# Float64 weights assembled with one more ScalarE pass and two VectorE passes, and zero products placed before TensorE work that the planner sees starting late

## The chip, the cores and the metric

The kernel runs on one NeuronCore of one Trainium2 chip. The metric is the device time of one execution in microseconds. TensorE (PE) multiplies matrices into PSUM, VectorE (DVE) and ScalarE (ACT) work elementwise on SBUF and PSUM, GpSimd (POOL) computes and issues indirect DMAs, SyncE (SP) issues most plain DMAs. Each engine takes its instructions in program order and waits for the others by semaphores.

## The reference, cut to what matters

```
# x (8,8,512,64), state (8,8,32,64) float32: attention in both directions
xread = softmax(x @ state.T / 8) @ state;  sread = softmax(state @ x.T / 8) @ x
x = concatenate([xread, sread])            # 8*544 = 4352 tokens of 512
# mixture of experts: 8 experts, each token goes to its best one
e = argmax(normed(x) @ normed(expert_emb).T / tau);  gate = softmax(...)[e]
x = gate * (relu(x @ w1[e]) @ w2[e])       # 512 -> 1024 -> 512
# dense feed-forward for every token; moe2_w_in and moe2_w_out come as float64
h = x @ w_in;  out = (h * clip(h + 3, 0, 6) / 6) @ w_out    # 512 -> 2048 -> 512
```

The two dense weights are float32 draws times a float64 number, so they reach the kernel as 8-byte values: each as two 32-bit words, `low` (low mantissa bits) and `top` (sign, 11 exponent bits, 20 mantissa bits).

## The kernel before, in words

The work has five stages: attention batch by batch with the router's logits; routing (which token goes to which slot of 128); a lead part with the five slots of the fullest expert; the other expert units, one or two slots each, interleaved with the dense feed-forward; and the rest of the feed-forward alone. Every matrix product outside the attention is made of three products: each operand is split into a rounded high part and the remaining low part (`wh`, `wl`; `xt` or `hx` twice; `yh`, `yw`; `gh`, `gl`).

**The planner.** Nothing is issued by hand: `op` records each piece of work with an engine, a cost in us, a priority (the time at which it is due), its dependences and the rings of buffers that it takes and gives back. `Sched.run` keeps a clock per engine (`clk`, "T" for TensorE) and picks the piece whose start `b`, plus a small weight on its priority, is lowest; then its function emits the instructions. The order on each queue is thus fixed at build time by the planner's costs, and on the chip every queue goes through its own list. A TensorE piece that follows a rest of over 2 us is costed longer for 3.4 us.

**The conversion of the float64 weights** (`Conv` and `convert`). There are 32 conversions, 16 pieces of w_in and 16 of w_out, 128 x 512 values each. Eight are in the attention (tiles `cv_raw` for the raw words, `cv_m` for the result), 24 later (the raw words in `cv_raw`, `yh` or `yw`; the result in a buffer of the ring `row`). One goes so: `load` (512 KB, issued by ACT's queue); `cv` (ACT, L295, takes three bits out of the low word); `ca` (DVE, L303 and L304, shifts the top word and takes its sign and exponent bit); `cq` (ACT, L312, squares the top word as float32); `cb` (DVE, L308, puts the three bits in); `cp` (DVE, L316, makes tiny values zero); `ch` (ACT, L324, rounded high part); `cl` (DVE or POOL, L327, low part). The buffer of the raw words and that of the result are both held until `cl`.

**The experts' weights** (`load_w`). A load (SP, L1232 or L1235) brings 512 KB into one of two `raw` buffers; each half is split by a cast `wh` (ACT or DVE, L1246) and a subtraction `wl` (DVE or POOL, L1249) into one of three pairs. The first layer (`h_ps`, `h_g`, L1410 and L1451) and the second (`y_ps`, `y_g`, L1513) multiply with them. A `raw` buffer takes its next load when both of its subtractions are done.

**TensorE elsewhere**: the warm-up `o_warm` (L511, 14 products of a float32 identity, before any data is there), transposes of x (`xT_ps`, L531), the routing's counting products (`rk_ps`, `pg_ps`, `pg_g`, L950 and L1066), transposes of the gathered tokens in the lead part (`m_g`, L1303), the feed-forward (`u_ps`, L1619; `o`, L1654).

Of the kernel before, what the change touches and what calls it, by code (L numbers as in the profile page):

```python
# [38 lines left out]
class Sched:  # L39
# [10 lines left out]
    def __init__(self):  # L50
        self.clk = dict.fromkeys("TADPS", 0.0)
        self.dma = self.hw = 0.0
        self.wp, self.port, self.cold = 0.0, 0.0, 0.0
        self.avail, self.n = [], 0

    def op(self, fn, cost, prio, deps=(), take=(), give=(), dma=0.0, after=None, port=""):

# [42 lines left out]
    def run(self, until=None):  # L100
        while self.avail and not (until and until()):
            best = None
            for o in self.avail:
                t, need = o.ready, {}
                for h in o.take:
                    for r in h.rings:
                        need[r] = need.get(r, 0) + 1
                for r, k in need.items():
                    if len(r.free) < k:
                        break  # L110
                    t = max(t, sorted(r.free)[k - 1])
# [12 lines left out]
            _, o, e, b = best  # L124
            self.avail.remove(o)
            for h in o.take:
                for r in h.rings:
                    r.free.remove(min(r.free))
            o.fn(e) if len(o.cost) > 1 else o.fn()
            c = o.cost[e]  # L130
            if e == "T":
                if b - self.clk["T"] > self.REST:
                    self.cold = b + self.COLD
                c += min(max(self.cold - b, 0.0) / 2, c)
            self.clk[e] = b + c
            if e in o.port:
                self.port = self.clk[e]
            end = self.clk[e] + self.SEEN[e]
            if o.dma:
                if e != "P":  # L140
                    self.hw = b + 0.45 * (1 + o.cost[e] // 0.12)
                self.dma = max(self.dma, self.clk[e] + self.LAT[e]) + o.dma
                end = self.dma + 1.2
            for h in o.give:
                h.readers -= 1
                h.until = max(h.until, end)
                if not h.readers:
# [7 lines left out]
def kernel(  # L155
# [87 lines left out]
    copy = {"A": ACT.copy, "D": DVE.tensor_copy}  # L243


    NRAW, NW, NROW, NGX = 2, 3, 6, 4
    NAX, NXT, NSC, NE2, NE1, NA2, NAH, NXR = (3, 3, 1, 1, 2, 1, 1, 1)
    NHX = 4
# [18 lines left out]
    class Conv:  # L267
# [3 lines left out]

        def __init__(self, w, m):
            self.w, self.m = w, m
            src = w_in if w == "i" else w_out
            self.wide = src.dtype != F32
            self.src, self.n = (src.bitcast(I32), 2) if self.wide else (src, 1)

        def load(self, pool):  # L280
# [7 lines left out]
            if self.wide:  # L288
                v = t.rearrange("p (f w) -> p f w", w=2)
                self.low, self.top = v[:, :, 0], v[:, :, 1]  # L290

        def cv(self):

            if self.wide:
                ACT.activation(self.low, self.raw.bitcast(U16).rearrange("p (f w) -> p f w", w=4)[:, :, 1], AF.Relu,  # L295
                               bias=seven[:, 0:1], scale=-(2.0**-13))

        def ca(self, pool):
            self.ma = self.raw
            if self.wide:  # L300
                t = self.bits = pool().bitcast(I32)
                self.ma = t.bitcast(F32)
                DVE.tensor_scalar(t, self.top, 3, 0x3FFFFFFF, op0=ALU.logical_shift_left, op1=ALU.bitwise_and)  # L303
                DVE.scalar_tensor_tensor(t, self.top, -0x40000000, t, op0=ALU.bitwise_and, op1=ALU.bitwise_or)  # L304

        def cb(self):
            if self.wide:
                DVE.scalar_tensor_tensor(self.bits, self.low, 7, self.bits, op0=ALU.bitwise_xor, op1=ALU.bitwise_or)  # L308

        def cq(self):  # L310
            if self.wide:
                ACT.activation(self.top.bitcast(F32), self.top.bitcast(F32), AF.Square)  # L312

        def cp(self, e="P"):
            if self.wide:
                eng[e].scalar_tensor_tensor(self.ma, self.top.bitcast(F32), (1.0625 * 2.0**-15)**2, self.ma,  # L316
                                            op0=ALU.is_ge, op1=ALU.mult)

        def ch(self):
            m = self.m  # L320
# [8 lines left out]
    conv = [Conv(*c) for c in conv_q]  # L329
    last_conv, dense = [None], {}  # L330

    def convert(n, prio, pool, ma, gate=None, start=0.0):
# [12 lines left out]
        g = op(c.ch, {"A": 0.55}, prio, [f, home])  # L345
        dense[conv_q[n]] = op(*((lambda: c.cl("P"), {"P": 1.26}) if early else (c.cl, {"D": 0.6, "P": 1.26})), prio, [g], (), [hr, hc], port="DP")
        if early:
            lead_ops.append(dense[conv_q[n]])

# [9 lines left out]
    pa = actx.enter_context(tc.tile_pool(name="a_ps", bufs=4, space=PSUM))  # L359

    def ps(name):
        return pa.tile([128, 2, 512], F32, tag="ps", name=name)


    BA = B - 2
# [695 lines left out]
    def o_pg(i):  # L1061
        n, k = SLOTS[i], 4 if i else 2
        p = pool["g_ps"].tile([128, 512], F32, tag="g", name="pg_g") if i else ps("pg_ps")[:, 0, :]
        p = V["pg", i] = p[:, 0:k * n].rearrange("p (a s) -> p a s", a=k)
        for j in range(NTILE):
            PE.matmul(p, V["bt", j], V["at", i][:, 0:k, :, j], start=j == 0, stop=j == NTILE - 1)  # L1066
# [316 lines left out]
            lead_ops.extend([og, o1, o2, u.x[-1]])  # L1383

    def ptile(u, name):
        return pool["g_ps"].tile([128, 512], F32, tag="g", name=name + "_g") if u.lead else \
            pool["pm"].tile([128, 512], F32, tag="m", name=name + "_ps")

    PARTS3 = ((0, "hi"), (0, "lo"), (1, "hi"))

    def L1w(u, k, prio, hf=0):
# [12 lines left out]
        def mm():  # L1404
            if new:
                u.hp[q] = [ptile(u, "h") for _ in u.h[q]]
            for c in range(2):
                for f in range(2):
                    for i, (a, w) in enumerate(PARTS3):
# [28 lines left out]
    def L1(u, k, prio):  # L1438
# [7 lines left out]
        def mm():  # L1446
            if k % 4 == 0:
                u.hp[v] = ptile(u, "h")
            for c in range(2):
                for i, (a, w) in enumerate(PARTS3):  # L1450
                    PE.matmul(u.hp[v][:, 256 * (q % 2):256 * (q % 2) + 256], u.xt[a][:, 2 * j + c, :],  # L1451
# [36 lines left out]
    def L2(u, c, prio, ii=None):  # L1488
# [13 lines left out]
        def mm():  # L1502
            if c == 0:
# [3 lines left out]
                else:  # L1507
                    y = pool["py"].tile([128, 2, DM], F32, tag="y", name="y_ps")
                    for i in ii:
                        u.y[i] = y[:, i, :]  # L1510
            for i in ii:
                for k, (a, w) in enumerate(PARTS3):
                    PE.matmul(u.y[i], u.ht[t][:, a, lo + 128 * i:lo + 128 * i + 128], pc[w],  # L1513
# [94 lines left out]
    def F1(i, m, prio, deps=()):  # L1608
# [3 lines left out]

        def mm():
            p = q["p"] = pool["pu"].tile([128, 256], F32, tag="u", name="u_ps")
            yh, yw = o["y"]
            for k in range(KD):
                wh, wl = (w[:, m % (KFF // 2), k, :] for w in wi_t[m // (KFF // 2)])
# [24 lines left out]
    def F2(i, m, prio, deps=()):  # L1642
# [5 lines left out]
        def mm():  # L1648
            if m == 0:
                o["o"] = [pool["po"].tile([128, DM], F32, tag=f"o{a}", name=f"o{a}") for a in range(2)]  # L1650
            woh, wol = (w[:, m % (KFF // 2), :] for w in wo_t[m // (KFF // 2)])
            for a in range(2):
                for j, (g, w) in enumerate(((q["h"], woh), (q["h"], wol), (q["l"], woh))):
# [7 lines left out]
        for a in range(2):  # L1661
# [3 lines left out]
            def scale(a=a, box=box):  # L1665
                t = box["t"] = pool["row"].tile([128, W], F32, tag="row", name="yo")[:, 0:DM]
                if a:
                    DVE.tensor_scalar(t, o["o"][1], 1.0 / 6, None, op0=ALU.mult)  # L1668
# [204 lines left out]
```

## Time and profile before

| | us |
|---|---|
| median of 3 runs (lowest, highest) | 1447.35 (1445.01, 1447.62) |
| profiled execution, whole | 1445.17 |
| its span, first to last instruction | 1443.5 |
| busy: PE, DVE, ACT, POOL | 1349.8, 907.5, 588.5, 421.0 |
| mean granted TensorE clock | 0.961 of full |

The profile is of one execution. Its times start at the first instruction of the span; 1.7 us lie around the span. A granted clock of 1.00 is TensorE's 2.4 GHz level, 0.50 the 1.2 GHz level, and a value between is a stretch with some of each. "Idle before" is how long an engine had nothing running before an instruction, followed by what ended that. An engine's busy time counts an instruction from start to end, so overlapping ones count once.

### The profile page before, as it was taken

The numbers are of one execution on the slowest core, as the hardware profiler recorded it, in microseconds if no ns is written. First come the engines' busy times: TensorE is split into PE (matmuls) and PEld (weight loads), VectorE is DVE, ScalarE is ACT, GpSimd is POOL, SyncE is SP. The second block draws the span as 40 slices with busy tenths as digits, with TensorE's granted clock in tenths as the row PEclk, the third lists the DMA queues.
The fourth block names the chain that finished last, engine by engine and source line by source line (L and its number), as shares of the span: only waits on it lengthen the run. The fifth ranks groups of instructions, "written<-read, shape, count | busy, mean of one in ns | idle before, by whom it ended". The sixth has DMA issues, their size and how long they took to land. (4 is left out here: it accounts for less than half of the span.)

```text
span 1443.5 us, 24914 instructions
## 1 busy us (share of the span) xinstructions
PE 1349.8 (94%) x8912; PEld 1194.9 (83%) x8912; DVE 907.5 (63%) x2102; ACT 588.5 (41%) x1276; POOL 421.0 (29%) x445
## 2 busy tenths in 40 slices
PE   7985797877899999999999999999999999999997
PEld 5764676775789899888989898998989999899996
DVE  6987876978865555545555545777756676434332
ACT  4764524555433243433334343333434444323332
POOL 4432546313252241413133133333333311100000
PEclk8997788999899999999999999999999999999999
DMA  6654336556454333333324233554545544101000
GB/s 161 182 168 144 123 103 179 181 169 189 132 176 145 106 102 112 112 109 97 117 89 125 89 111 110 161 154 159 163 135 156 167 142 152 46 23 30 15 16 15
DMA packets 151762, 175.60 MB, mean 122 GB/s; under 512 B 43784, under 2 KB 116488, under 8 KB 150608
## 3 DMA queue, kind: packets, MB, share of 16 engines
q1 hardware_dynamic: 128544, 121.19, 28.0%
q0 software_dynamic: 12336, 35.99, 8.2%
q10 hardware_dynamic: 10752, 16.78, 3.6%
q8 instruction: 71, 1.16, 0.3%
q14 instruction: 59, 0.48, 0.1%
HBM read 146.09 MB, written 27.82 MB: 120 GB/s over the span
## 5 line engine op out<-in xcount | busy, mean ns | idle before, releaser
L1619 PE MATMUL u_ps<-yh,wih 128*128 128x256 f32 x1088 | 305.6, 281 | 1.0 <-PEq L1828 0.9
L1619 PE MATMUL u_ps<-yw,wih 128*128 128x256 f32 x1088 | 305.7, 281 | 0.5 <-DVE yw L1598 0.5
L1619 PE MATMUL u_ps<-yh,wil 128*128 128x256 f32 x1088 | 305.2, 281 | 0.0
L1623 ACT ACTIVATE r<-u_ps,three 128x256 f32<-128x256 f32 x272 | 129.0, 474 | 347.5 <-PE u_ps L1619 343.3
L1626 DVE SCALAR_TENSOR_TENSOR u_ps<-r,u_ps 128x256 f32<-128x256 f32 x272 | 116.4, 428 | 223.4 <-ACT r L1623 223.1
L1654 PE MATMUL o<-woh,gh 128*128 128x512 f32 x544 | 216.7, 398 | 1.6 <-DVE yo L1668 1.3
L1654 PE MATMUL o<-wol,gh 128*128 128x512 f32 x544 | 215.9, 397 | 0.0
L1619 PEld LDWEIGHTS u_ps<-yh,wih 128*128 128x128 f32 x1088 | 205.7, 189 | 10.8 <-DVE gl L1633 2.2
L1654 PE MATMUL o<-woh,gl 128*128 128x512 f32 x544 | 214.4, 394 | 0.0
L1619 PEld LDWEIGHTS u_ps<-yw,wih 128*128 128x128 f32 x1088 | 205.0, 188 | 8.7 <-DVE yw L1598 0.7
L1619 PEld LDWEIGHTS u_ps<-yh,wil 128*128 128x128 f32 x1088 | 205.6, 189 | 0.0
L1249 DVE TENSOR_TENSOR wl<-raw,wh 128x512 fp32r<-128x512 f32 x272 | 191.1, 712 | 9.2 <-ACT wh L1246 4.7
L1630 ACT CAST gh<-u_ps 128x256 fp32r<-128x256 f32 x272 | 101.3, 372 | 211.7 <-PE o L1654 168.7
L1633 DVE TENSOR_TENSOR gl<-u_ps,gh 128x256 fp32r<-128x256 f32 x272 | 114.8, 422 | 112.7 <-ACT gh L1630 112.3
L1513 PE MATMUL y_ps<-wh,hx 128*128 128x512 f32 x512 | 184.5, 397 | 0.0
L1249 POOL TENSOR_TENSOR wl<-raw,wh 128x512 fp32r<-128x512 f32 x80 | 109.5, 1369 | 252.2 <-DVE wh L1246 122.8
L1277 POOL DMA_INDIRECT xq<-xd,qidx x128 | 130.4, 1018 | 79.0 <-DVE xt L1330 44.0
L1410 PE MATMUL h_ps<-xt,wh 128*128 128x256 f32 x704 | 145.9, 297 | 0.8 <-ACT wh L1246 0.6
L1246 DVE CAST wh<-raw 128x512 fp32r<-128x512 f32 x232 | 100.6, 436 | 63.2 <-PE y_ps L1513 23.0
L1410 PE MATMUL h_ps<-xt,wl 128*128 128x256 f32 x352 | 105.6, 300 | 27.8 <-DVE wl L1249 23.0
L1673 POOL DMA_INDIRECT out_dram<-yo,ix x34 | 37.5, 1104 | 311.1 <-DVE yo L1668 215.7
L1410 PEld LDWEIGHTS h_ps<-xt,wh 128*128 128x128 f32 x704 | 122.3, 206 | 2.8 <-ACT wh L1246 0.8
(299 smaller groups left out, 2262.1 us busy)
## 6 DMA issues: line engine op xcount, KB each, us to landing
raw<-in_moe_w_dram SPq DMA_DIRECT2D x176, 512.0 KB, 3.9
yl<-ysd SPq DMA_DIRECT2D x136, 64.0 KB, 2.6
xd<-xr SPq DMA_DIRECT2D x8, 1056.0 KB, 4.8
ysd<-yt POOLq DMA_DIRECT2D x32, 256.5 KB, 3.1
xb<-in_x_dram SPq DMA_DIRECT2D x48, 128.0 KB, 3.1
yw<-in_moe_w_out_dram ACTq DMA_DIRECT2D x9, 512.0 KB, 4.0
cv_raw<-in_moe_w_in_dram ACTq DMA_DIRECT2D x8, 512.0 KB, 5.5
yh<-in_moe_w_in_dram ACTq DMA_DIRECT2D x8, 512.0 KB, 4.9
```

What stands on the lines that cost most here:

```text
L1246: copy[e](pc["hi"], box["t"][:, j, :])
L1249: eng[e].tensor_tensor(pc["lo"], box["t"][:, j, :], f32(pc["hi"]), op=ALU.subtract)
L1277: POOL.indirect_dma_start(q[:, j * QW:(j + 1) * QW], None, xd_q, index(qidx[:, j, s:s + 1]))
L1410: PE.matmul(out(f), pc[w][:, (2 * c + f) * 128:(2 * c + f + 1) * 128], u.xt[a][:, 2 * j + c, 256 * hf:256 * hf + 256], start=new and c == ...
L1513: PE.matmul(u.y[i], u.ht[t][:, a, lo + 128 * i:lo + 128 * i + 128], pc[w], start=c == 0 and k == 0, stop=c == KF - 1 and k == 2)
L1619: PE.matmul(p, w, y[:, k, :], start=k == 0 and j == 0, stop=k == KD - 1 and j == 2)
L1623: ACT.activation(q["r"], q["p"], AF.Relu, bias=pool["three"][:, 0:1])
L1626: DVE.scalar_tensor_tensor(q["p"], q["r"], 6.0, q["p"], op0=ALU.min, op1=ALU.mult)
L1630: ACT.copy(q["h"], q["p"])
L1633: DVE.tensor_tensor(q["l"], q["p"], f32(q["h"]), op=ALU.subtract)
L1654: PE.matmul(o["o"][a], g[:, a * 128:(a + 1) * 128], w, start=m == 0 and j == 0, stop=m == KFF - 1 and j == 2)
L1673: POOL.indirect_dma_start(out, bass.IndirectOffsetOnAxis(ap=o["ix"][:, a:a + 1], axis=0), box["t"], None)
```

## The change

There are two parts. The first changes how a float64 weight becomes float32. ScalarE multiplies the top word, read as float32, by 2^-111 (`cg`), takes the three bits as before (`cv`) and turns them round by a second pass (`cw`); VectorE puts the sign bit to them (`ca`), and then the shifted top word (`cb`). The square, the mask and the product that zeroed tiny values are gone. Weights come out 256 times too large, which is undone in the scale of the Relu and in the last scaling. The raw buffer is given back after `cb`, the result's buffer is taken there. The second part gives TensorE products of zeros: `busy` reads how far the planner sees the piece's start after the end of the TensorE piece before it (`gap`), and emits one 128x128x128 bf16 product of zeros for each 0.055 us of that beyond 0.5 us, if it is over 1 us, up to 160. They stand after the claim of the PSUM tile and ahead of the piece's own products, written into columns that these overwrite (`start=True`), or added to sums that exist (`start=False`). `none` is every second 16-bit word of the float32 identity, all zero. The warm-up gets 70 such products.

```diff
@@ Sched.run
+            self.gap = b - self.clk["T"] if e == "T" else 0.0
             o.fn(e) if len(o.cost) > 1 else o.fn()
@@
+    none = ident.bitcast(BF16).rearrange("p (c t) -> p c t", t=2)[:, :, 0]
+    def busy(p, start=True):
+        gap, sc.gap = sc.gap, 0.0
+        n = min(int((gap - 0.5) / 0.055), 160) if gap > 1.0 else 0
+        for _ in range(n):
+            PE.matmul(p[:, 0:128], none, none, start=start, stop=start)
@@ class Conv
+        def cg(self):
+            if self.wide:
+                ACT.activation(self.top.bitcast(F32), self.top.bitcast(F32), AF.Copy, scale=2.0**-111)
...
+        def cw(self):
+            if self.wide:
+                ACT.activation(self.low, self.low, AF.Copy, bias=7.0, scale=-1.0)
+        def ca(self):
+            if self.wide:
+                DVE.scalar_tensor_tensor(self.low, self.top, -0x80000000, self.low, op0=ALU.bitwise_and, op1=ALU.bitwise_or)
-        def ca(self, pool):
+        def cb(self, pool):
             self.ma = self.raw
             if self.wide:
-                t = self.bits = pool().bitcast(I32)
+                t = pool().bitcast(I32)
                 self.ma = t.bitcast(F32)
-                DVE.tensor_scalar(t, self.top, 3, 0x3FFFFFFF, op0=ALU.logical_shift_left, op1=ALU.bitwise_and)
-                DVE.scalar_tensor_tensor(t, self.top, -0x40000000, t, op0=ALU.bitwise_and, op1=ALU.bitwise_or)
-        def cb(self):
-                DVE.scalar_tensor_tensor(self.bits, self.low, 7, self.bits, op0=ALU.bitwise_xor, op1=ALU.bitwise_or)
-        def cq(self):
-                ACT.activation(self.top.bitcast(F32), self.top.bitcast(F32), AF.Square)
-        def cp(self, e="P"):
-                eng[e].scalar_tensor_tensor(self.ma, self.top.bitcast(F32), (1.0625 * 2.0**-15)**2, self.ma,
-                                            op0=ALU.is_ge, op1=ALU.mult)
+                DVE.scalar_tensor_tensor(t, self.top, 3, self.low, op0=ALU.logical_shift_left, op1=ALU.bitwise_or)
@@ convert
-        v = op(c.cv, {"A": 0.55}, prio, [a])
-        b = op(lambda: c.ca(ma), {"D": 0.96}, prio, [a], [hc], port="D")
-        q = op(c.cq, {"A": 0.55}, prio, [b])
-        b = op(c.cb, {"D": 0.61}, prio, [b, v], port="D")
-        f = op(lambda: c.cp("D"), {"D": 0.6}, prio, [b, q], port="D")
+        v = op(c.cv, {"A": 0.66}, prio, [a])
+        v = op(c.cw, {"A": 0.57}, prio, [v])
+        b = op(c.cg, {"A": 0.57}, prio, [a])
+        b = op(c.ca, {"D": 0.61}, prio, [b, v], port="D")
+        f = op(lambda: c.cb(ma), {"D": 0.61}, prio, [b], [hc], [hr] if c.wide else (), port="D")
@@ o_warm
+        for _ in range(70):
+            PE.matmul(p[:, 0, 0:128], none, none, start=True, stop=True)
@@ busy(...) is called where a PSUM tile is claimed: ps, o_pg, ptile, L2, F1 and
@@ (with start=False) before products that add to one: L1w, L1, L2, F2
@@ scales
-            ACT.activation(q["r"], q["p"], AF.Relu, bias=pool["three"][:, 0:1])
+            ACT.activation(q["r"], q["p"], AF.Relu, bias=pool["three"][:, 0:1], scale=unit_i)
-                    ACT.activation(t, o["o"][0], AF.Copy, scale=1.0 / 6)
+                    ACT.activation(t, o["o"][0], AF.Copy, scale=unit_i * unit_o / 6)
```

## Rows read from the trace of the kernel before

**Rows 1.** The page, its first part: busy time, share and instructions.

```profile
PE 1349.8 (94%) x8912; PEld 1194.9 (83%) x8912; DVE 907.5 (63%) x2102; ACT 588.5 (41%) x1276; POOL 421.0 (29%) x445
```

**Rows 2.** Windows: length, busy time by engine, granted clock, DMA share, GB/s.

```profile
200.00:420.00 220.00, 180.55 (x978) 157.95 (x978) 173.82 (x377) 106.32 (x220) 85.80 (x84) 0.88 0.57 171
420.00:1244.00 824.00, 818.61 (x5231) 737.92 (x5230) 506.26 (x1175) 315.35 (x721) 252.32 (x242) 1.00 0.41 126
```

**Rows 3.** Waits of PE, 160 to 420: us in total, times, longest.

```profile
PE h_ps L1410 <- DVE wl L1249: 23.0, 7, 5.8
PE y_ps L1513 <- DVE wl L1249: 7.2, 2, 6.7
PE h_ps L1410 <- POOL wl L1249: 4.5, 1, 4.5
PE y_g L1513 <- DVE wl L1249: 3.3, 1, 3.3
```

**Rows 4.** Timeline of DVE before the longest wait: start, us, instruction.

```profile
329.24 0.43 DVE L303 TENSOR_SCALAR cv_m<-yw 128x512 int32<-128x512 int32 x1
...
335.11 0.69 DVE L316 SCALAR_TENSOR_TENSOR cv_m<-yh,cv_m 128x512 f32<-128x512 f32 x1
...
335.72 0.69 DVE L1249 TENSOR_TENSOR wl<-raw,wh 128x512 fp32r<-128x512 f32 x1
```

**Rows 5.** Timeline of PE, the longest of five rests behind conversions.

```profile
336.46 0.80 PE L1513 MATMUL y_ps<-wl,hx 128*128 128x512 f32 x1 [6.68 <-DVE wl L1249]
```

**Rows 6.** The conversion's lines: count, duration in ns least/median/most, first and last start.

```profile
L303 DVE TENSOR_SCALAR cv_m<-cv_raw x14: 404/420/596, 44.3 to 238.9; 128x512 int32<-128x512 int32 x14
L304 DVE SCALAR_TENSOR_TENSOR cv_m<-cv_raw,cv_m x14: 691/694/1652, 44.7 to 239.3; 128x512 int32<-128x512 int32 x14
L312 ACT ACTIVATE cv_raw<-cv_raw x14: 653/684/700, 45.7 to 241.2; 128x512 f32<-128x512 f32 x14
```

**Rows 7.** Waits of SP's queue, 200 to 420, columns as in group 3.

```profile
SPq L1232 <- DVE wl L1249: 77.9, 13, 16.0
```

**Rows 8.** DMA issues, 200 to 420: count, KB each, median us to landing.

```profile
raw<-in_moe_w_dram SPq DMA_DIRECT2D x30, 512.0 KB, 4.9
```

**Rows 9.** Windows of stretches at the low clock, columns as in group 2.

```profile
9.22:19.46 10.24, 6.53 (x34) 4.87 (x35) 4.61 (x6) 2.84 (x6) 6.59 (x13) 0.50 0.95 191
...
135.52:162.83 27.31, 11.52 (x73) 9.60 (x74) 20.66 (x89) 14.21 (x39) 13.10 (x15) 0.50 0.49 162
...
193.54:203.78 10.24, 10.24 (x44) 7.11 (x42) 4.36 (x11) 1.28 (x2) 2.71 (x4) 0.50 0.41 129
...
227.68:234.50 6.82, 5.57 (x13) 4.41 (x14) 6.65 (x11) 2.60 (x5) 3.61 (x4) 0.50 0.23 64
...
415.41:418.82 3.41, 3.41 (x18) 3.41 (x18) 1.45 (x3) 0.60 (x1) 0.00 (x0) 0.50 1.01 309
```

**Rows 10.** Timeline of PE at the front; x24 is the number of products.

```profile
1.49 5.43 PE L511 MATMUL warm<-ident 128*128 128x128 f32 x28 [1.49 <-POOL ident masks.py:199]
12.26 0.59 PE L442 MATMUL enT_ps<-ident,em 8*128 8x8 f32 x4 [5.33 <-DVE em L439]
...
14.68 3.68 PE L531 MATMUL xT_ps<-ident,xb 128*128 128x128 f32 x16
...
27.15 2.96 PE L531 MATMUL xT_ps<-ident,xb 128*128 128x128 f32 x24 [0.55 <-DVE xb L505]
```

**Rows 11.** Waits of PE, 0 to 160.

```profile
PE m_g L1303 <- ACT xp L1298: 11.7, 4, 5.5
...
PE pg_ps L1066 <- DVE at L1059: 3.4, 1, 3.4
PE rk_ps L950 <- DVE hsum L946: 2.9, 1, 2.9
```

**Rows 12.** Timeline of PE: the routing's two bf16 product groups, in which PE waits for nothing.

```profile
139.92 2.31 PE L1066 MATMUL pg_ps<-at,bts 128*128 128x10 bf16 x34 [3.38 <-DVE at L1059]
...
189.53 10.17 PE L1066 MATMUL pg_g<-at,bts 128*128 128x164 bf16 x34
```

More of the change, by code (lines that the diff above doesn't have):

```diff
@@ L53, in __init__ @@
         self.wp, self.port, self.cold = 0.0, 0.0, 0.0
-        self.avail, self.n = [], 0
+        self.avail, self.n, self.gap = [], 0, 0.0
     def op(self, fn, cost, prio, deps=(), take=(), give=(), dma=0.0, after=None, port=""):
@@ L296, in cv @@
                                bias=seven[:, 0:1], scale=-(2.0**-13))
-        def ca(self, pool):
+        def cw(self):
[5 more added lines that the diff above has]
+        def cb(self, pool):
             self.ma = self.raw
             if self.wide:
-                t = self.bits = pool().bitcast(I32)
+                t = pool().bitcast(I32)
                 self.ma = t.bitcast(F32)
-                DVE.tensor_scalar(t, self.top, 3, 0x3FFFFFFF, op0=ALU.logical_shift_left, op1=ALU.bitwise_and)
-                DVE.scalar_tensor_tensor(t, self.top, -0x40000000, t, op0=ALU.bitwise_and, op1=ALU.bitwise_or)
-        def cb(self):
-            if self.wide:
-                DVE.scalar_tensor_tensor(self.bits, self.low, 7, self.bits, op0=ALU.bitwise_xor, op1=ALU.bitwise_or)
-        def cq(self):
-            if self.wide:
-                ACT.activation(self.top.bitcast(F32), self.top.bitcast(F32), AF.Square)
-        def cp(self, e="P"):
-            if self.wide:
-                eng[e].scalar_tensor_tensor(self.ma, self.top.bitcast(F32), (1.0625 * 2.0**-15)**2, self.ma,
-                                            op0=ALU.is_ge, op1=ALU.mult)
+                DVE.scalar_tensor_tensor(t, self.top, 3, self.low, op0=ALU.logical_shift_left, op1=ALU.bitwise_or)
         def ch(self):
@@ L330 @@
     last_conv, dense = [None], {}
+    unit_i, unit_o = (1.0 if t.dtype == F32 else 2.0**-8 for t in (w_in, w_out))
     def convert(n, prio, pool, ma, gate=None, start=0.0):
@@ L339, in convert @@
         a.ready = start
-        v = op(c.cv, {"A": 0.55}, prio, [a])
-        b = op(lambda: c.ca(ma), {"D": 0.96}, prio, [a], [hc], port="D")
-        q = op(c.cq, {"A": 0.55}, prio, [b])
-        b = op(c.cb, {"D": 0.61}, prio, [b, v], port="D")
-        f = op(lambda: c.cp("D"), {"D": 0.6}, prio, [b, q], port="D")
+        v = op(c.cv, {"A": 0.66}, prio, [a])
[3 more added lines that the diff above has]
+        f = op(lambda: c.cb(ma), {"D": 0.61}, prio, [b], [hc], [hr] if c.wide else (), port="D")
         g = op(c.ch, {"A": 0.55}, prio, [f, home])
-        dense[conv_q[n]] = op(*((lambda: c.cl("P"), {"P": 1.26}) if early else (c.cl, {"D": 0.6, "P": 1.26})), prio, [g], (), [hr, hc], port="DP")
+        dense[conv_q[n]] = op(*((lambda: c.cl("P"), {"P": 1.26}) if early else (c.cl, {"D": 0.6, "P": 1.26})), prio, [g], (),
+                              [hc] if c.wide else [hr, hc], port="DP")
         if early:
@@ L361, in ps @@
     def ps(name):
-        return pa.tile([128, 2, 512], F32, tag="ps", name=name)
+        p = pa.tile([128, 2, 512], F32, tag="ps", name=name)
+        busy(p[:, 0, :])
+        return p
     BA = B - 2
@@ L1063, in o_pg @@
         p = pool["g_ps"].tile([128, 512], F32, tag="g", name="pg_g") if i else ps("pg_ps")[:, 0, :]
+        busy(p)
         p = V["pg", i] = p[:, 0:k * n].rearrange("p (a s) -> p a s", a=k)
@@ L1385, in ptile @@
     def ptile(u, name):
-        return pool["g_ps"].tile([128, 512], F32, tag="g", name=name + "_g") if u.lead else \
+        p = pool["g_ps"].tile([128, 512], F32, tag="g", name=name + "_g") if u.lead else \
             pool["pm"].tile([128, 512], F32, tag="m", name=name + "_ps")
+        busy(p)
+        return p
     PARTS3 = ((0, "hi"), (0, "lo"), (1, "hi"))
@@ L1406, in mm @@
                 u.hp[q] = [ptile(u, "h") for _ in u.h[q]]
+            busy(u.hp[q][0][:, 0:256], False)
             for c in range(2):
@@ L1448, in mm @@
                 u.hp[v] = ptile(u, "h")
+            busy(u.hp[v][:, 0:256], False)
             for c in range(2):
@@ L1510, in mm @@
                         u.y[i] = y[:, i, :]
+                    busy(u.y[0])
+            busy(u.y[ii[0]], False)
             for i in ii:
@@ L1614, in mm @@
             p = q["p"] = pool["pu"].tile([128, 256], F32, tag="u", name="u_ps")
+            busy(p)
             yh, yw = o["y"]
@@ L1650, in mm @@
                 o["o"] = [pool["po"].tile([128, DM], F32, tag=f"o{a}", name=f"o{a}") for a in range(2)]
+            busy(o["o"][0], not m)
             woh, wol = (w[:, m % (KFF // 2), :] for w in wo_t[m // (KFF // 2)])
@@ L1667, in scale @@
                 if a:
-                    DVE.tensor_scalar(t, o["o"][1], 1.0 / 6, None, op0=ALU.mult)
+                    DVE.tensor_scalar(t, o["o"][1], unit_i * unit_o / 6, None, op0=ALU.mult)
                 else:
-                    ACT.activation(t, o["o"][0], AF.Copy, scale=1.0 / 6)
+                    ACT.activation(t, o["o"][0], AF.Copy, scale=unit_i * unit_o / 6)
             def put(a=a, box=box):
```

## The prediction

> **What bounds the kernel now.** I read the page's busy times first: PE is at work 94% of the span [rows 1], so 1443.5 - 1349.8 = 94 us are its idle time. Windows then show where: from 420 to 1244 it is busy 818.6 of 824 us at full clock, so nothing can be won there, while from 200 to 420 it is idle 39.4 us, its granted clock is 0.88, and DVE is busy 174 of 220 us [rows 2]. The list of PE's waits names the cause: 38.0 us in 11 rests, 160 to 420, all for `wl`, the low part of an expert's weight [rows 3]. The timeline of DVE shows what stands ahead of such a `wl`: in the longest rest the eight operations of two conversions, from 329.24 to 335.80, and then `wl` at 335.72 [rows 4], after which PE goes on at 336.46, having rested 6.68 us [rows 5]. Five rests have conversions right ahead of the late `wl`: those that end at 228.93, 311.19, 336.46, 361.51 and 382.44 (the longest is shown), with one, two, two, one and one and a half conversions in them. A third loss follows each rest: the granted clock is at the 1.2 GHz level in eight stretches between 227 and 419, the first (227.68) and last (415.41) of which are shown [rows 9]; the eight together last 47.8 us and hold 39.0 us of PE work.
>
> **Part one, the conversion.** Before, DVE spends 0.42 on L303 and 0.69 each on L304, L308 and L316: 2.49 us [rows 4, 6]. After, two operations of the form of L304 remain: 1.38. So 1.11 us of DVE go per conversion, 26.6 us over the 24 that run from 192 to 382, and 8.9 over the eight of the attention. ACT loses one pass (L312, 0.68) and gets two of like form: 0.7 more, 17 us over the 24. I cost that at nothing, since ACT is busy 106 of 220 us there [rows 2]; were its cover gone, 17 us. The three ACT passes now run one after the other without DVE between them, so one round trip goes. ACT's queue also issues the conversions' loads, which stand 0.7 us further back. The raw buffer is given back before cast and subtraction (0.6 and 0.7 us earlier), and nothing on the path waited for that.
>
> What are 26.6 us of DVE worth to PE? At least what stands right ahead of a late `wl`: 7.5 conversions by 1.11 = 8.3 us. At most all of it, 26.6, as the 38 us of rests could take it. Against the upper end speaks what is late next: SP's queue waits 77.9 us on `wl` to issue loads of `raw` [rows 7], and a load lands 4.9 us after issue [rows 8], so an earlier `wl` soon meets a load. I take 13, nearer to the lower end.
>
> In the attention PE has few rests, and the routing's chain on DVE holds some conversions; of 8.9 us I take 2 (0 to 8.9).
>
> **Part two, the zeros.** The 70 of the warm-up start at 6.9, when the 14 products end [rows 10], and the next PE work is at 12.26 [rows 10], with the clock low from 9.22 to 19.46 [rows 9]. At 0.055 to 0.068 each (below) they end between 10.8 and 11.7: before that work, and close enough that the clock should hold. Then 16 transposes that take 3.68 us, 0.230 each, take the 0.123 of later ones (24 in 2.96) [rows 10]: 1.7 us, and some tenths in the products around them. PE is the bound from 14 on, so I take 2 (at most 3.3, half of the 6.53 us of work in that low stretch [rows 9]; below, see the slower rival).
>
> The low stretch of 135.52 to 162.83 holds 11.5 us of PE work [rows 9], 5.8 us of it excess. Rests of 11.7, 3.4 and 2.9 us lie in it or before it, six in all [rows 11], and are of a kind that a planner foresees, since a chain of single steps makes them. But PE is not the bound before 159, so only the last transposes and first products count: 2 (0 to 5.8).
>
> In the eight low stretches 39.0 us of work lose 19.5. After part one about a third of the 38 us of rests is gone, so 13 of excess remain; the plan won't foresee all rests, since it prices DVE's `wl` at 0.6 and the trace at 0.69 [rows 4], and a faster PE meets the next weight sooner. I take half, 6.5 (0 to 19.5).
>
> What does a zero cost? It has its own weight load. The nearest rows: bf16 products with own weight load and ten columns follow each other every 2.31 / 34 = 0.068 us at the low clock [rows 12], so the load is no longer than that; transposes of 128 columns with own load, float32, 0.123 at full clock [rows 10]. The other bf16 group, 10.17 / 34 = 0.30 for 164 columns [rows 12], has columns 68 bytes apart; the zeros' are 4 apart, as float32 ones are. I take 0.055 to 0.068. The foreseeable rests are the 11 of [rows 3] and the six of [rows 11]: 56.0 us, less 0.5 each is 47.5 us of zeros by the plan's price. At 0.068 they take 58.7, an overrun of 2.7 us, nothing. Where no rest was foreseen, nothing is added; PE's stretch from 420 on has hardly any. Claiming the PSUM tile ahead of the zeros adds no wait, since the piece behind them claims it anyway.
>
> The Trainium skill ("TensorE: Matmul & The Clock Gate", section Back-to-back issue gap) says that a stream of pairs of weight load and 128-column product sustains about 81 ns per product. By it the zeros would take 47.5 x 81 / 55 = 70 us, an estimated overrun of 14, and the sum would come to 1435; no row here shows such a pair in bf16, and rival (e) below is that case. Its page "SBUF — State Buffer" (section Specifications, Cachelines) charges a read that crosses to a new 16-byte line each time; the group with 68-byte steps agrees with its 0.30 us, and by that page the zeros' steps would cost nothing.
>
> **The sum.** 13 + 2 + 2 + 2 + 6.5 = 25.5 us. Against the profiled execution, 1445.2 as a whole (1443.5 of span and 1.7 around), that gives 1419.7; the runs' median is 2.2 higher, which would make 1421.9. I say 1421.
>
> **The rivals.** (a) The loads of `raw` take the place of DVE: part one gives 4 and the clock 3 between 160 and 420, the other three terms 6, so 13 in all: 1433. For it speaks SP's queue [rows 7]; against it, that ahead of the longest rest's end DVE is never without work [rows 4]. Chance 0.16. (b) All counts: 26.6 from DVE, 12 from the clock, 8 from the rest: 47, 1399. For it speaks that rest, DVE and clock have one cause. Chance 0.16. (c) Few rests are foreseen, so that only DVE's part in both stages and the front remain: 17, 1429. Against it, the planner's costs know rests (a surcharge follows those over 2 us). Chance 0.12. (d) The slower side: the zeros are longer than the plan's 0.055, and PE comes to its real work late. They are, if a pair costs the 0.123 of the transposes, or if zeros do not hold the clock and run at half of it, 0.110. The bf16 group at 189.53 speaks for the latter: it ran until 199 without a wait [rows 12], and the granted clock is 0.50 from 193.54 on [rows 9]. Then 47.5 us become 95 to 106, an overrun of 39 to 50 us; it outweighs the gain from (56.0 + 25.5) / 47.5 x 0.055 = 0.094 us per zero on. With 15 us from part one, none from the clock, and all of the overrun on the path, that is 1445 + 24 to 1445 + 35; as later rests take some of it, 1460. Chance 0.11. (e) A zero lies between the two rows, at some 0.08: 47.5 us become 69, 13 more than the rests hold, so 1434. Chance 0.08.
>
> **How the numbers follow.** The forecast has the remaining 0.37, its own range 1412 to 1429. Faster by over 0.2% (about 3 us, what a measurement of this kernel can tell from none) is nearly all of the forecast, (a), (b), (c) and (e): 0.84. Slower is most of (d) and a little of (a) and (e): 0.11; the same, 0.05. The range of 1396 to 1446 leaves out most of (d) and the lower part of (b), under 0.2.
>
> **What would show it.** Right: DVE's busy time down by some 35 us, ACT's up by some 22; of PE's 38 us of waits for `wl` some 25 left; L531's first group at 0.123 each; several of the eight low stretches gone, also that of 135 to 163; zeros at 0.055 to 0.07 each. Wrong: waits for `wl` as long as before with `wh` waiting on `raw` loads (a), few zeros outside the warm-up (c), zeros of over 0.09 us with real products starting right behind them although their operands were long ready (d). The forecast is wrong if PE's idle time and low clock between 160 and 420 shrink and the stretch from 420 on grows.

## The result, and the profile after

1432.76 us is the median after (1430.82 to 1435.97), beside 1446.18 before in the same series: the ratio is 0.991 [0.9887, 0.9933]. The gain of 13.4 us is half of the forecast's 26, with the sign that was forecast. The page's first part, after:

```profile
PE 1367.9 (96%) x9533; PEld 1215.3 (85%) x9533; DVE 868.0 (61%) x2037; ACT 607.7 (43%) x1313; POOL 416.0 (29%) x441
```

Against [rows 1] DVE has 39.5 us less, ACT 19.2 more (35 and 22 were said); PE has 621 more products, the zeros among them. The conversion's lines answer to [rows 6]; columns are count, duration in ns least/median/most, first and last start:

```profile
L307 ACT ACTIVATE cv_raw<-cv_raw x14: 652/667/698, 37.3 to 221.2; 128x512 f32<-128x512 f32 x14
L317 ACT ACTIVATE cv_raw<-cv_raw x14: 653/668/700, 37.8 to 221.8; 128x512 int32<-128x512 int32 x14
L321 DVE SCALAR_TENSOR_TENSOR cv_raw<-cv_raw x14: 629/684/690, 42.7 to 223.3; 128x512 int32<-128x512 int32 x14
L328 DVE SCALAR_TENSOR_TENSOR cv_m<-cv_raw x14: 628/683/1420, 43.4 to 224.2; 128x512 int32<-128x512 int32 x14
```

L321 and L328 are the two bit operations, 0.68 us each, L307 and L317 two of ScalarE's three passes, 0.67 each: the sizes of part one were right. The windows that answer to [rows 9] and [rows 2] (length, busy time by engine, granted clock, DMA share, GB/s):

```profile
9.22:19.46 10.24, 8.42 (x97) 6.21 (x95) 4.79 (x7) 2.74 (x6) 6.60 (x13) 1.00 0.96 197
135.52:162.83 27.31, 25.20 (x287) 24.27 (x286) 21.54 (x83) 18.01 (x47) 15.68 (x16) 0.88 0.47 148
200.00:420.00 220.00, 193.34 (x1278) 169.51 (x1277) 156.05 (x358) 119.94 (x251) 84.16 (x86) 0.95 0.60 176
420.00:1244.00 824.00, 816.23 (x5245) 736.23 (x5244) 497.21 (x1151) 315.66 (x720) 243.69 (x234) 1.00 0.42 124
```

The clock did what was expected: 0.50 became 1.00 at the front and 0.88 in the routing's stretch, and 0.88 became 0.95 from 200 to 420. But PE's busy time now holds the zeros, so its 12.8 us more from 200 to 420 are no measure of work done. PE's waits, 160 to 420, answer to [rows 3]:

```profile
PE u_ps L255 <- DVE gl L1659: 5.9, 2, 5.4
PE h_ps L1432 <- DVE wl L1268: 5.6, 6, 1.6
PE u_ps L255 <- DVE yt L1562: 4.3, 1, 4.3
PE u_ps L1645 <- ACT yh L1620: 4.1, 1, 4.1
PE y_ps L1538 <- DVE wl L1268: 2.4, 3, 1.0
```

Of the 38.0 us of waits for `wl` 9.0 are left (some 25 were said). In their place stand waits of the dense layer's first product (`u_ps`), 14.3 us in three rows, where the kernel before had 0.7. Two of the rows are on L255, the zeros' line: a zero waits there, and the timeline of PE shows what follows (start, us, instruction, idle time before it in brackets):

```profile
317.28 7.23 PE L255 MATMUL u_ps<-ident 128*128 128x128 bf16 x96 [5.43 <-DVE gl L1659]
324.32 0.36 PE L1645 MATMUL u_ps<-yh,wih 128*128 128x256 f32 x1
...
352.21 6.06 PE L255 MATMUL u_ps<-ident 128*128 128x128 bf16 x82 [4.31 <-DVE yt L1562]
358.08 0.36 PE L1645 MATMUL u_ps<-yh,wih 128*128 128x256 f32 x1
```

PE rests for the PSUM tile first (at 352.21 too: `gl`, which frees it, ends 0.05 us earlier, together with the short copy `yt` that the row names), and then, with the tile free, works through 96 and 82 zeros before the product that it rested for. The zeros stand behind the rest that they were counted for, not in it.

### The profile page after: what moved, and what is told of

The parts are those of the page before. It is cut to its first block, busy times and chain, and to the rows that moved or that the text cites. A ratio compares the mean times of both kernels' runs of the same rounds, so it can differ in the third digit from the quotient of the medians.

```text
span 1429.2 us, 26063 instructions
## 1 busy us (share of the span) xinstructions
PE 1367.9 (96%) x9533; PEld 1215.3 (85%) x9533; DVE 868.0 (61%) x2037; ACT 607.7 (43%) x1313; POOL 416.0 (29%) x441
## 5 line engine op out<-in xcount | busy, mean ns | idle before, releaser
L1268 DVE TENSOR_TENSOR wl<-raw,wh 128x512 fp32r<-128x512 f32 x277 | 196.2, 718 | 8.5 <-ACT wh L1265 3.9
L1268 POOL TENSOR_TENSOR wl<-raw,wh 128x512 fp32r<-128x512 f32 x75 | 105.1, 1402 | 232.2 <-DVE wh L1265 125.2
L1432 PE MATMUL h_ps<-xt,wh 128*128 128x256 f32 x704 | 135.8, 282 | 2.3 <-DVE wh L1265 2.3
L1681 PEld LDWEIGHTS o<-woh,gl 128*128 128x128 f32 x544 | 102.1, 188 | 25.0
L1681 PEld LDWEIGHTS o<-woh,gh 128*128 128x128 f32 x544 | 102.1, 188 | 20.0 <-DVE yo L1695 2.5
```

Of the source, the lines that this page charges most:

```text
L1268: eng[e].tensor_tensor(pc["lo"], box["t"][:, j, :], f32(pc["hi"]), op=ALU.subtract)
L1432: PE.matmul(out(f), pc[w][:, (2 * c + f) * 128:(2 * c + f + 1) * 128], u.xt[a][:, 2 * j + c, 256 * hf:256 * hf + 256], start=new and c == ...
L1681: PE.matmul(o["o"][a], g[:, a * 128:(a + 1) * 128], w, start=m == 0 and j == 0, stop=m == KFF - 1 and j == 2)
```

## The experiments

Five readings were on trial. C: zeros behind a claim run after the rest and only delay (L, its rival: the experts' loads bound that stretch anyway). P: 10 us come and go with a shift of a few us, whatever the edit. D: the conversion's gain is VectorE's time. R: it is the buffer that comes free sooner. A: ScalarE's time counts as well. Each ratio is to the kernel before, timed in the same series. There were four series, each on a chip of its own: the first four experiments, the next four, then the three from the late release to the 105 zeros, and the 85 zeros by themselves. The kernel before took 1442.3, 1446.9, 1445.7 and 1443.2 us in them.

**Without F1's zeros**

```diff
-            busy(p)
+            sc.gap = 0.0
```

> The changed kernel without zeros ahead of the feed-forward's first layer (F1); all others stay. Theory C (claim): those zeros run only after the claimed PSUM tile is free, when the rest is over, so the two large groups (from 317.28 and 352.21, 7.0 and 5.9 us) are pure delay: 1420 us (1418 to 1426), the first PE product after each claim starting right behind the claim. Theory L (loads): after 300 PE follows the experts' weight loads, so an earlier F1 only waits longer at the next weight: 1433 us (1430 to 1435).

Measured: 1422.3 us, 0.9847 [0.9821, 0.9872]. The 192 zeros of F1 (the feed-forward's first layer, `u_ps`) cost 0.0063 of 1446, 9 us. The same two products in its trace:

```profile
315.98 0.55 PE L1645 MATMUL u_ps<-yh,wih 128*128 128x256 f32 x1 [5.26 <-DVE gl L1659]
...
347.76 0.58 PE L1645 MATMUL u_ps<-yh,wih 128*128 128x256 f32 x1 [6.00 <-DVE yt L1562]
```

They start 8.3 and 10.3 us earlier than after, and the span ends 8.5 earlier (1420.7 beside 1429.2). C holds, L falls.

**The conversion alone**

```diff
-        n = min(int((gap - 0.5) / 0.055), 160) if gap > 1.0 else 0
-        for _ in range(n):
-            PE.matmul(p[:, 0:128], none, none, start=start, stop=start)
...
-        for _ in range(70):
-            PE.matmul(p[:, 0, 0:128], none, none, start=True, stop=True)
```

> The changed kernel without any zeros, warm-up included: the new conversion alone, in the changed kernel's order. Theory C: the conversion gives about what I forecast for it, 13 to 17 us, and the zeros give about as much as they cost: 1431 us (1428 to 1434). Theory L: the conversion gives 4 to 7 us and the zeros the rest: 1440 us (1438 to 1443).

Measured: 1422.9 us, 0.9861 [0.9834, 0.9887]. All of the gain, and more, is the conversion's: 20 us here, over the 13 to 17 of C and far over the 4 to 7 of L.

**The zeros alone** (the old `Conv`, every `busy`)

> The zeros with the old conversion, in the order of the kernel before. Theory C: front and routing give 4 to 5 us, the filled rests some clock, and zeros behind claims take part of it back: 1442 us (1438 to 1446). Theory L: 7 to 9 us faster, 1438 us.

Measured: 1443.6 us, 1.0011 [0.9993, 1.003]: nothing. Yet the granted clock from 200 to 420 was 0.93 there, 0.88 before [rows 2], and PE's busy time 14.5 us more. So I read it that what the zeros gave back in clock they took as work; no run separates the two.

**The conversion and the warm-up's 70 zeros**

```diff
-        n = min(int((gap - 0.5) / 0.055), 160) if gap > 1.0 else 0
-        for _ in range(n):
-            PE.matmul(p[:, 0:128], none, none, start=start, stop=start)
```

> The new conversion and the 70 zeros of the warm-up, no others. Both theories: 1.5 to 2 us less than the conversion alone, since the first 16 transposes take 1.97 instead of 3.68 us and PE is the bound behind them.

Measured: 1421.6 us, 0.985 [0.9825, 0.9875]. This version, the conversion alone and the one without F1's zeros are the fastest, within one another's intervals, and beat both kernels.

**F1's zeros twice**

```diff
+            g = sc.gap
+            busy(p)
+            sc.gap = g
             busy(p)
```

> The changed kernel with twice the zeros ahead of each F1. Theory C (claim): the zeros behind a claim are delay one for one, so the time grows by about what taking them away saved, 9 to 13 us: 1442 us where the changed kernel has 1433. Theory P (placement): taking them away only let the later work fall better by chance; then doubling moves the time by under 4 us.

Measured: 1454.7 us, 1.0056 [1.0037, 1.0074], 21 us more than after. The two products that start at 324.32 and 358.08 after start here at

```profile
336.99 0.36 PE L1648 MATMUL u_ps<-yh,wih 128*128 128x256 f32 x1
...
375.62 0.36 PE L1648 MATMUL u_ps<-yh,wih 128*128 128x256 f32 x1
```

12.7 and 17.5 us later. P, which allowed under 4 us, falls as far as this place goes; but 21 us are more than the 9 to 13 of C. The first of the two groups shows one reason:

```profile
319.60 6.13 PE L255 MATMUL u_ps<-ident 128*128 128x128 bf16 x73 [5.24 <-DVE gl L1662]
326.11 0.39 PE L255 MATMUL u_ps<-ident 128*128 128x128 bf16 x4 [0.38 <-issue]
327.57 0.33 PE L255 MATMUL u_ps<-ident 128*128 128x128 bf16 x3 [1.07 <-issue]
329.02 8.16 PE L255 MATMUL u_ps<-ident 128*128 128x128 bf16 x112 [1.12 <-issue]
```

PE rested 2.6 us within the 192 zeros, for nothing that the trace names, and the granted clock fell to 0.57 behind these rests (330 to 334), so that the 192 took 17.4 us to the product behind them; the 164 of the second group took 10.7. After they were 7.0 and 5.9. The zeros are delay, but not in proportion to their number; the other reason follows with the table below.

**Warm-up and only the zeros added to sums that exist**

```diff
-            busy(p)
...
-            busy(u.hp[q][0][:, 0:256], False)
+            if not new:
+                busy(u.hp[q][0][:, 0:256], False)
...
-                    busy(u.y[0])
-            busy(u.y[ii[0]], False)
+            if c:
+                busy(u.y[ii[0]], False)
```

(so at every claim, and at the first product of a sum)

> The new conversion, the 70 zeros of the warm-up, and only those other zeros that are added to sums that exist, which claim nothing. If the zeros of the routing (behind claims, and about one us longer than the rest they fill) are worth nothing, this is as fast as conversion and warm-up alone, 1421 us, give or take 2. If they were worth the 2 us that I forecast, it is 2 us slower than the changed kernel without F1's zeros: 1424.

Measured: 1431.7 us, 0.9889 [0.9869, 0.9909]: a miss, 56 zeros seem to cost 6 us; the table below places the loss elsewhere.

**F1's zeros ahead of the claim**, added to the open sums of `o`

```diff
+            if opened_o[0] is not None:
+                busy(opened_o[0], False)
...
-            busy(p)
...
+            opened_o[0] = o["o"][0] if m < KFF - 1 else None
```

> The changed kernel with F1's zeros moved ahead of the claim, added to the second layer's open sums. Theory C: they now run while PE would wait for the PSUM tile, so they cost nothing and keep the clock: 1420 us (1417 to 1424), the two large groups inside the rests, and the low clock behind those rests gone. Theory P: no different from the zeros where they were, 1432.

Measured: 1435.9 us, 0.9928 [0.9911, 0.9944]: a second miss. But at the place itself the trace shows what C foretold:

```profile
311.29 5.68 PE L255 MATMUL o<-ident 128*128 128x128 bf16 x96
317.09 0.36 PE L1647 MATMUL u_ps<-yh,wih 128*128 128x256 f32 x1
...
344.51 4.88 PE L255 MATMUL o<-ident 128*128 128x128 bf16 x82
349.19 0.36 PE L1647 MATMUL u_ps<-yh,wih 128*128 128x256 f32 x1
```

No rest is left, and the products start 1.1 and 1.4 us after those of the kernel without F1's zeros. The loss lies elsewhere. Where, one comparison tells: in all kernels with the new conversion each engine but PE has exactly the same instructions in the same order (the late release aside, and the doubled operations), and PE the same but for zeros. So the start of ScalarE's n-th instruction in one trace minus its start in another, each counted from the start of its span, is the lag at that point. In us, against the conversion with 70 zeros, at that trace's times:

```
time there           37.0  188.3  218.2  219.4  306.2  325.0  364.6  395.8  487.6  end
no zeros             +2.6   +3.3   +3.2   +3.2   +3.9   +3.9   +4.7   +4.0   +5.2   +2.5
warm-up 85            0.0   +0.1   +0.5   +0.5   +0.9   +1.5   +1.3   +0.8   +0.1   +4.9
warm-up 105          +0.4   +0.1   +2.1   +4.5   +5.7   +5.7   +5.1   +6.3  +13.3  +12.5
without F1's zeros   +0.8   +2.0   +2.1   +2.1   +2.6   +2.5   +2.2   +1.6   +3.5   +1.8
after                +0.8   +0.7   +1.2   +1.2   +4.0   +7.8   +9.8   +9.3   +9.8  +10.4
F1's zeros twice     +0.8   +0.2   +1.3   +4.3   +6.3  +20.4  +27.4  +27.4  +33.4  +33.3
sums only            +1.4   +1.5   +1.4   +4.5   +3.5   +3.4   +1.7   +1.8  +10.0  +13.1
F1's zeros ahead     +0.8    0.0   +0.5   +4.3   +3.6   +4.3   +4.4   +5.0  +12.7  +15.9
```

F1's zeros, read from 306 to 365: +5.8 after, +21.1 twice, -1.8 to +0.8 in the six kernels that leave them out or have them ahead. The 15 us between once and twice are what the two groups take longer (17.4 - 7.0 and 10.7 - 5.9). The other 8 of the 23 us by which the doubled kernel ends later lie at 219 and between 396 and 488, and the two misses lose 8 us in that last stretch as well, where no zero runs. There ScalarE's `r`, the Relu of `u_ps`, comes late; first in the conversion with 70 zeros, then with the zeros ahead:

```profile
412.83 0.28 PE L1642 MATMUL u_ps<-yh,wil 128*128 128x256 f32 x1
413.15 0.47 ACT L1646 ACTIVATE r<-u_ps,three 128x256 f32<-128x256 f32 x1 [4.21 <-PE u_ps L1642]
```

```profile
418.36 0.28 PE L1647 MATMUL u_ps<-yh,wil 128*128 128x256 f32 x1
422.45 0.47 ACT L1651 ACTIVATE r<-u_ps,three 128x256 f32<-128x256 f32 x1 [8.35 <-PE u_ps L1647]
423.76 0.51 PE L1538 MATMUL y_ps<-wh,hx 128*128 128x512 f32 x1 [2.35 <-DVE wh L1265]
```

With 70 zeros `r` starts 0.03 us after the last product that it reads has ended, here 3.8 us after it; PE's rest for `wh` comes behind that.

**VectorE's last operation of a conversion twice**

```diff
-                DVE.scalar_tensor_tensor(t, self.top, 3, self.low, op0=ALU.logical_shift_left, op1=ALU.bitwise_or)
+                for _ in range(2):
+                    DVE.scalar_tensor_tensor(t, self.top, 3, self.low, op0=ALU.logical_shift_left, op1=ALU.bitwise_or)
```

> Conversion and warm-up zeros alone, with the last VectorE operation of each conversion done twice: 0.69 us more of DVE per conversion, 16.6 us over the 24 behind the attention and 5.5 in it, in the same order. Theory D (what the conversion gained is DVE's time): 35.5 us of DVE gave some 19, so 22 us take back about 12: 1433 us. Theory R (it gained by the earlier release of buffers and by fewer turns between DVE and ACT): under 4 us more, 1425 or less.

Measured: 1448.4 us, 1.0012 [0.9999, 1.0025]: 22 us more on DVE (890.7 beside 868.8) made 23. The lag grows evenly with the conversions, 5.9 at 216, 12.7 at 282, 19.8 at 396, and to 26.2 at 488 by the loss named above, with no doubled operation there. D, at 19.8 / 21.9 = 0.9 us for 1 us, where 12 for 22 were expected.

**Late release of the raw buffer**

```diff
-        f = op(lambda: c.cb(ma), {"D": 0.61}, prio, [b], [hc], [hr] if c.wide else (), port="D")
+        f = op(lambda: c.cb(ma), {"D": 0.61}, prio, [b], [hc], port="D")
...
-                              [hc] if c.wide else [hr, hc], port="DP")
+                              [hr, hc], port="DP")
```

> The conversion with the 70 zeros of the warm-up and no others, and the buffer of a converted block (raw, cv_raw and the like) is not given back by the operation that assembles the number (cb) but, as in the kernel before, by the last step of the block (cl). The plan is made anew with that, so the order on the engines may move. Theory D (the gain of the conversion is VectorE's time, and nothing else): no change beside the same kernel with the early release, 0.985 (about 1422 us, 1417 to 1427). Rival R (the gain comes from the buffer that comes free earlier, so that the next block's load starts earlier): most of the gain is lost, 0.995 or more (1438 us and up).

Measured: 1427.1 us, 0.9874 [0.9847, 0.9901]; the plan's order changed with it. That is 3.5 us from the early release by the ratios, with intervals that overlap, and not the 16 or more of R, which falls.

**ScalarE's copy of the high half twice**

```diff
-            ACT.copy(self.hi, self.ma)
+            for _ in range(2):
+                ACT.copy(self.hi, self.ma)
```

> The conversion with the 70 zeros of the warm-up and no others, and ScalarE's copy of the high half of each of the 32 blocks (ch, 0.62 us) is done twice: 32 x 0.62 = 19.8 us more on ScalarE, as much as the conversion's own multiplication and offset put there; no order changes. Theory D (VectorE sets the rests, ScalarE has room): at most 4 us lost, 0.985 to 0.988 (1422 to 1426 us). Rival A (any engine of the chain raw to weights counts the same, so the move to ScalarE gave back part of the gain): 10 to 20 us lost, 0.992 to 0.999.

Measured: 1440.1 us, 0.9957 [0.9941, 0.9973]. 17.9 us more on ACT (625.0 beside 607.1) cost 15 us; VectorE's lag grows evenly, 4.9 at 201, 10.5 at 275, 15.9 at 383 and 15.3 at 396, 0.85 for 1 us (then to 22.4 at 488 by that loss). A holds, though ACT was busy 121.3 of the 220 us from 200 to 420 without the second copy.

**105 zeros in the warm-up**

```diff
-        for _ in range(70):
+        for _ in range(105):
```

> The conversion with 105 zeros in the warm-up instead of 70, and no others: 35 x 0.0575 = 2.0 us more ahead of the first transpose, nothing else, and no order changes. By the plain reading (a delay of TensorE at the front is carried to the end) 2 us later than with 70: 0.9865 (1424 us, 1421 to 1427). By the rival of the two kernels whose zeros ran in their rests and which yet came out 5 to 9 us slower (a shift of a few us alone makes the loads of the last expert blocks meet other transfers, at some 415 us, and costs several us more there): 0.989 or more (1428 us and up), with a wait for raw or wl at 410 to 425 us.

Measured: 1432.8 us, 0.9919 [0.9902, 0.9936]. That is 10 us over the kernel with 70 zeros, without one zero in the working part, as P foretold. Until 188 us this trace is with the one of 70 zeros to 0.4 us, then it falls back 2 us by 218, 2.5 at one copy of ScalarE, and 7 between 396 and 488. That copy, with 70 and with 105 zeros:

```profile
219.40 0.62 ACT L1262 CAST wh<-raw 128x512 fp32r<-128x512 f32 x1
```

```profile
223.91 0.62 ACT L1262 CAST wh<-raw 128x512 fp32r<-128x512 f32 x1 [2.41 <-issue]
```

In the table the four kernels whose copy comes 2.5 to 3.8 us later against its neighbour are the four that lose 6 to 8 us from 396 to 488; the four others lose at most 2. But the loss does not need the late copy: of the two kernels with a doubled operation, which are not in the table, ScalarE's has both (3.2 us late, 7.2 lost), while VectorE's has its copy on time (0.3) and loses 6.4. What all six that lose there share is the late `r`: it starts 1.8 to 4.3 us after the product that it reads, and a second one near 450 on the time scale of the 70 zeros 4.7 to 6.1 us after, where the five others, the kernel with 70 zeros among them, have 0.03 to 0.1.

P is not shown by that. The six lag 0.0 to 1.4 us at 37, the five others 0.0 to 2.6, so the shift does not sort them. The series does: the six are all that ran in the second and third series with this order of instructions, and none of the others did. Their traces also hold fewer semaphore events, some 13,100 to 13,400, than those of the five others, some 15,700. No kernel was run in series of both kinds, so whether the 10 us are the 35 zeros' or come with the chip, which the ratio to the kernel before may not cancel, stays open.

**85 zeros in the warm-up**

```diff
-        for _ in range(70):
+        for _ in range(85):
```

> The conversion with 85 zeros in the warm-up, between the 70 (1421.6 us, 0.985) and the 105 (1432.8 us, 0.9919) that came out 10 us apart though all engines' orders are the same; 15 x 0.0575 = 0.9 us more than with 70. If the time of the conversion alone follows the front's delay, 0.985 to 0.988. If two families of executions of one order stand side by side (in the profile with 105 one copy of ScalarE at 219 us starts 2.4 us late, in that with 70 it does not), the time is that of the one or the other, 0.985 or 0.992, and the copy at 219 us tells which: on time with the first, 2 to 4 us late with the second.

Measured: 1425.4 us, 0.9883 [0.986, 0.9905]: a time between the two, so the two families are not borne out by it. The copy is on time and the loss from 396 to 488 is absent, as with 70; but at 37 us the lag is 0.0, so this run moved nothing there either. The profiled execution lost 3.6 us behind 1190, with the clock at the lower level once.

What holds the copy back is not settled: the trace names nothing ("issue"), and the last load of `raw` issued ahead of it had landed by 217.5. Nor is it shown why `r` comes late; PE had gone on to the products behind by then.

## Why the prediction was right in sign and half in size

**The conversion: 15 forecast, 12 to 22 measured.** Alone it stands in four kernels, at 0.9861, 0.985, 0.9883 and 0.9919; the mean, 0.9878, is 17.6 us (three of the four have the warm-up's zeros too, and the last has the loss of its series; without it they are 17 to 22). So the sum is nearly right, but two of its steps were wrong and made up for each other: that it came out is luck. "I take 13, nearer to the lower end": VectorE's time is worth 0.9 us for 1 us, so its 35.5 us (32 conversions by 1.11) count nearly in full, 32. "I cost that at nothing" was said of ScalarE: its time counts 15.3 / 17.9 = 0.85 for 1, so its 19.2 us take 16 back. The difference, an estimate from the two lags at 396, is 16 us, 19 with the 39.5 us that VectorE lost in the trace. (The reading of the longest rest left out that four subtractions `xt` ran on VectorE between its two conversions, 1.42 us of the 6.56.) An engine that is busy half of a stretch was taken for one with room; but `wh`, `wl`, `yh`, `yt` and `hx` go back and forth between the two engines in a fixed order, and in both experiments the longer operation of either delayed all behind it.

What is late next was named wrongly too: "so an earlier `wl` soon meets a load". SP's queue issues the loads from two lines, of which [rows 7] shows one. The other one before, and both after:

```profile
SPq L1235 <- DVE wl L1249: 49.6, 11, 12.9
```

```profile
SPq L1254 <- DVE wl L1268: 57.5, 10, 15.1
SPq L1251 <- DVE wl L1268: 55.0, 9, 11.7
```

So it waits 112.5 us on `wl` from 200 to 420, 127.5 before: less than it did. Nor do the casts `wh` wait much longer on loads, 11.7 us after and 11.1 before on ScalarE and VectorE together. Next come the dense layer's products, here in the conversion alone with 70 zeros, which rival (a) did not see:

```profile
PE u_ps L1642 <- DVE yt L1559: 6.2, 1, 6.2
PE u_ps L1642 <- DVE gl L1656: 6.1, 2, 5.6
PE u_ps L1642 <- ACT yh L1617: 5.2, 1, 5.2
PE h_ps L1429 <- DVE wl L1265: 4.7, 8, 1.6
```

Rival (a) has the measured time, 1433, by loads that did not become the bound. Rival (c) is partly true: the plan made 248 zeros from 200 to 420 and 275 in the routing, 29 us by its price, and not the 47.5 of the prediction. The attention's term of 2 held: the first product of `y_g` comes 2.9 us earlier, and the next 11.6 us are won before the first of `u_ps`, in the kernel before and in the conversion alone:

```profile
203.80 0.39 PE L1513 MATMUL y_g<-wh,hx 128*128 128x512 f32 x1
...
262.42 0.28 PE L1619 MATMUL u_ps<-yh,wih 128*128 128x256 f32 x1
```

```profile
200.94 0.39 PE L1533 MATMUL y_g<-wh,hx 128*128 128x512 f32 x1
...
247.96 0.58 PE L1640 MATMUL u_ps<-yh,wih 128*128 128x256 f32 x1 [5.60 <-ACT yh L1615]
```

**The warm-up: 2 forecast, 2.5 in the trace of the conversion with it beside the one without.** PE at the front, after, beside [rows 10]:

```profile
7.17 4.18 PE L529 MATMUL warm<-ident 128*128 128x128 bf16 x70
12.61 1.21 PE L255 MATMUL stT_ps<-ident 128*128 128x128 bf16 x18
15.05 1.97 PE L549 MATMUL xT_ps<-ident,xb 128*128 128x128 f32 x16
```

The 16 transposes take 0.123 each. The conversion without any zeros lags 2.6 us from 37 on, and 2.5 at the end; by the medians it is 1.6, within their intervals. After, with the 18 zeros at 12.61 that the plan added, 0.8 of it is lost again by 37.

**Routing 2, clock 6.5: nothing.** From 102 to 188 the lag of the kernel after stays at 0.7 to 0.9, though 275 zeros run there and the clock rises. In the low stretches the step "I take half, 6.5", half of the excess that was to be left, failed: the clock of 200 to 420 is 0.96 with the conversion and no zero at all, 0.95 after. It came back with the conversion, as the rests for `wl` went, and the zeros added nothing to that.

**The zeros' price: right at full clock, and not what mattered.** 70 in 4.18 us after, and 96 in 5.68 and 82 in 4.88 with the zeros ahead, are 0.060 each at a granted clock of 1.00, inside 0.055 to 0.068. After, behind the rest, the same 96 and 82 took 7.04 and 5.87 us to the product behind them, 0.073 and 0.072 each, over that range, at a granted clock of 0.76 and 0.78. Rivals (d) and (e) by price, over 0.09 and some 0.08, fall even so. The Trainium skill ("TensorE: Matmul & The Clock Gate", section Back-to-back issue gap) has some 81 ns for such a pair in a stream; the trace does not agree here, and the measurement decides.

**The step that failed with a price:** "Claiming the PSUM tile ahead of the zeros adds no wait, since the piece behind them claims it anyway." It adds no wait, but puts the zeros behind it: two groups of 7.0 and 5.9 us, behind which the products start 8.3 and 10.3 us later, and 8.5 us are left of that at the end by the table's traces without and with them (+1.8, +10.4), 9 by the ratios. That is rival (d)'s sign and its mark, real products right behind zeros, with another cause.

The sum as measured: 17 to 22 for the conversion and the warm-up, less 9 for F1's zeros, is 8 to 13; 13.4 came out.

## What to carry over

Filler work that is to fill a rest must stand ahead of the wait that makes the rest, in the engine's order; behind it, it is a delay, which doubling shows at once (ahead of it, here, it cost little and won nothing). Where two engines hand work to and fro in a fixed order, time moved from one to the other is priced on both, whatever their busy shares. Before a difference of under 1% is put down to an edit, time the two kernels side by side on one chip, since a ratio to a third kernel may not cancel what differs between series; and compare traces instruction by instruction where the order is the same, for that shows where the difference lies.

## What the runs showed that was not expected

The kernel with 105 zeros in the warm-up came out 10 us slower than the one with 70 (0.985 and 0.9919, intervals apart), with no instruction moved on any engine and the front 0.4 us later; the one with 85 is at 0.9883. As the three ran in three series, this is not shown to be the zeros' doing. Ahead of the late copy one thing differs between the traces of 70 and 105. With 70 zeros a load of `raw` is issued at 211.10, 0.4 us after a gather (210.69); its packets run ahead of the gather's, and it has landed by 214.5, 3.4 us after issue. With 105 it is issued at 212.99, 0.9 us after the gather (212.11); its packets run behind the gather's, and it has landed by 217.5, 4.5 us after issue. That this is what sets off the rest was not shown.
